# A written-out order for four engines: new tables for the middle of a Conformer block on one core

## The chip, the core and the metric

The kernel runs on one core of a Trainium2 chip. The core has five engines that run at the same time, each through its own list of instructions: TensorE (PE, matrix multiplies into PSUM), VectorE (DVE), ScalarE (ACT, the exponentials and tanh), GpSimd (POOL) and SyncE (SP, which issues transfers). They wait for each other only through semaphores. The metric is the device time of one execution, in microseconds (us). Before the change it is 867.25 us, the median of 3 runs (867.09 to 867.63).

## The reference, cut to what matters

Two sequences of 4000 tokens with 144 features go through one Conformer block: feed-forward, self-attention with 4 heads of 36, gated convolution, feed-forward, and a layer norm in front of each part and at the end.

```
x = x + 0.5 * (silu(layernorm(x) @ w_ff1a) @ w_ff1b)
q, k, v = split(layernorm(x) @ w_qkv)              # 4 heads of 36
p = softmax(q k^T / 6)                             # 4000 x 4000 for each head and sequence
x = x + (p v) @ w_o
a, b = split(layernorm(x) @ w_pw1)
c = depthwise 5-tap convolution of a * sigmoid(b)  # zeros beyond both ends
x = x + silu(c) @ w_pw2
x = x + 0.5 * (silu(layernorm(x) @ w_ff2a) @ w_ff2b)
return layernorm(x)
```

The exponentials of the scores are the largest part: 2 sequences x 4 heads x 4000 x 4000.

## The kernel before

**Tiles of attention.** Queries are taken in 16 chunks of 500, keys in steps of 64 (the last one has 32). One tile is one key step of one chunk, all four heads; there are 1008 of them, 16 of which are the short rests. The scores of a tile are four matmuls of 64x64 weights against 500 columns (`scores`, rows `PS<-QT,KT` of the profile); each uses one quarter of the array and four of them run side by side. They fill two PSUM banks. An exponential turns both banks into a bf16 tile `PT`, and four more matmuls (`PS<-PT,VA`) sum it with the values into the two banks `BX` and `BX + 1`, where column 37 is the sum of the softmax.

**Two ways to an exponential.** The letter of a tile in the table `TYPES` says who does it.

- `A`: one instruction on ACT over 1000 columns (`e_args`). `R` is the same for a rest, over 500 columns.
- `D`: DVE does it by bit arithmetic (`z_args`, `ymw_args`). Two instructions `z` of 500 columns turn scores into 16-bit integers whose high bits are the exponent. Then, over 1000 columns, `y` cuts out the mantissa, `m` multiplies, and `w` keeps the exponent. The tile becomes two buffers, `w` and `m`, and so eight matmuls with the values, not four.
- `W`: as `D`, with one `z` of 1000 columns.

Two such tiles can share `y`, `m` and `w`, each then of 2000 columns, where the table `PAIRS` names them. The long instruction starts when the `z` of both tiles are done.

**The other work.** For each chunk of 500 tokens there are the layer norms (statistics on DVE, `ST`; a scale-and-add of four numbers to a row, `RS<-ST`, on POOL or DVE; a power on POOL, `RS<-RS,NHALF`; the normalised rows `XN` on POOL, DVE or ACT), a transpose by a transfer (`XTB<-XN`), and full-array matmuls: feed-forward (`WA`, `WE`, `WB`), projections (`WQ`, `WK`, `WQKV`), output (`WO`), gate (`WP`, `WPZ`) and convolution (`DG`). Results leave PSUM through DVE or ACT: the copies `KT`, `QT`, `VA`; `HT` after a tanh on ACT; and the residual `X`. A residual on DVE is one instruction that adds to `X`. On ACT it is a plain copy, and two matmuls of `X` with an identity (`PS<-X,EYE`) add the old value before it.

**What sets the order.** Recording the program (`Rec.op`) yields blocks of instructions and their dependencies. `settle` then replaces all attention tiles by what the tables say, and `Rec.arrange` puts the blocks of each engine in exactly the order of the table `ORDER`, two characters for a block. The chip takes each engine's list in that order; an instruction that has to wait holds up all that stand behind it on its engine. The other tables:

- `UNITS`: one letter for each of 447 small pieces of work that more than one engine can do (`Rec.unit`, `Rec.choose`): `d` DVE, `a` ACT, `p` POOL.
- `BANKS`: the PSUM banks (0 to 5) of each tile. `PLACES`: the first bank of each other PSUM use.
- `SLOTS`: which of the 11 `PT` buffers each tile uses. A buffer or a bank is written again when its last reader, in PE's order, is through.

The order is thus made outside the kernel, by a search over a plan that gives each instruction a duration. What is in the kernel of that plan are the costs in `c_act`, `c_dve` and `c_pe`; the tables do not depend on them when the program is built.

```
def c_act(n):
    return n / 1200 + 0.0535
...
        R.choose(UNITS)
...
            m = lead.get(n)
            wide = () if m is None else tuple(parts[m][4])
...
        R.arrange(ORDER, readers, slots, users)
```

Of the kernel before, what the change touches and what calls it, by code (L numbers as in the profile page):

```python
# [13 lines left out]
H = 4  # L14
# [21 lines left out]
        '!!!#!$!%!&!(!+!)!*!,!-!.!/!0!1!3!6!2!;!5!4!<!=!7!8!A!9!:)c)d!@!>)g)h!B)l)k!?)p)o!C)w)x!D)t)s)r)m)n)e'  # L36
        ')|)i)j){!E!J!G!F!H*!)y)v)q)f)u!I!K!L!M!P!S!N!R!O!Q!T!U!`!V!W!b!X!Z!^!g!_!f!Y!d!j!a!c![*$*#!]!e!o!p!l'
        '!k!h*)*(!m*,*-!n)z*1*0!i!q*4*5*&*%*8*9!s!t*=*<)}*/*3*.*6*@*A!u!r!w!v*E*D!x*I*H!y*L*M*B*G*V*+*;*:*W*P'
        '*7*F*Q***2*K*Z*[*>*C*J!z*`*_!{!|!}*c*d*g*h#!##*q*?*m*n*T*U*}*Y*N*^*X*r#%#&*v*u*p*b*o#$*z*y*O*R+!*a*k'
        '*t+,+-*f*e#)+)+(*S*s#(+:+;+.*|*j*w+%*x+G*]+1+0+/+4*l*i#*+5*{+?+>+=+<+++F+B+C+*#+#,#-+L+M+Q+@+D+A+P+$'  # L40
        '+9+&+##.+[+Z+T+O+E+_+`+R+S+J+I+K+2+8+U+c+d+k+3+H+h+g+6+7+N+r+q#/+v+u+l+i+b+^+f+z+y+a,&+]+}+j,!+s+t+w'
        '+X,++e+x,%#0,1,0+{+Y,*,$+o+p,4,5#1,8,9+V#2,=,<,),2+m+W,G,#,7,F,A,@+n,:,3,6,K,J,(+|,>,;,/,,,N,O,H,S,I'
        ',.,R,-,?,Z#3,W,V,L,Q,M,P,b,a#4,f,e,[,X,U,T,Y,i,j#5,m,n,d,B,q,C,x,w#6,{,|,g,l,c,r-#-$#7-)-(,h,k,z-,,p'
        '-2-3,o#8-6-7,y-+-*,E-%-&-;-:,}-!,^,_,]---?->#9-C-B,u-K-<-9-=-8-F-G-4,`,D-1-P-Q,t-.,v-@-5-J-U-T-D-E-X'
        '-I-0-/-_-`-Y-A-H,s-d-c#<-g-h#:#;#>#?#=-k-l-o-b-p-e-f-w-j-N-W-i-V-O-t-s#@#A#B-x-a.!-}#C.&.%-L-S-R-M.*'
        '.+./-q-r.#-u-v...$#D#E.8.9-^.-.,.).<.=-]#F.@.A.;.3.:-m-n.D.E.0#G.1-{.I.H.2-z.>.?.(.L.M-|.P.Q-Z.K.B.^'
        '._-y.O.F-[.T.C.N.J.G.b.c.7.R.S.X.f.6.5.g.j.V.U.4.k.W#H#I.a.h.u.t.`.y.x.e.d.n.|.}#J.o.l.m.z/%.i/$.{/)'
# [12 lines left out]
        '56#{5=5%595:4_4o4^5D5C5>5350574n545/5X5W5<5G5+585N5M#|5F5`5;5H5Q5,5Y5Z5[5]5E5B5O5*5a5)#}5A5P5d5e5^5_'  # L60
        '5?5R5@5i5h$!5m5l$#5q5p5t5f5g6!5}5j5J5b5c5k5I5w6&6%5L5r5o5s5K5x5n5V5U6*6+5T5S5u5v$$6/6.6962$%686(636<'
        '6=$&$(6A6@6$6#6)$)6:6E6?6D656I666;6H$*61606S6R6,6C6L675z6B6W6V$+646M6F5|6Z6G6>6[6e6Y6U5{6f6X6_6-6T6K'
        '$,$-6j6i6^6m6g6]6n6N6O6J6h5y6`6P6w6x$.6q6p6{6Q6o6|6k6l6y6r7#7$$/7(7)$0$17-7,6}6b706d767!7%77$26a717&'
        '7.7;7:6v6u7>7E6z787/7D$37H7I7*7?797<7+6c7M7L$47Q7P7G7F6s6t7T7U$5$674757X7Y7]7S$77d7c7C7J7B7^7g7K7V7h'
        '7R7O7N737q7=7k7r$87v7u7f7i7j727e7l7z7y$97@7W8(8)7}7A7s7b7Z7[8,8-$:81807t7w8!7_7`8*8584$;8?8>83827p88'
        '7|7a8+8B8C7{$<8.8/8F8G8@89867x$=878J8K8D8A7o8&8N8E8H8U8T$>8X8Y7m8$8%8O8L8M8]8^$?8#8W7n8V8g8h8;8a8:8['
        '8Z8I8k8l$@8p8o8`8i8R8b8P8j8s8t$A8x8w8r8q$B8{9)9*8u8=8n9-8Q8<8y9.9!8v8S8m8|8}92918c8d8e8f8_8z96959#$C'
        '9?9@909/9C9D9,99$D9H9G94939:97989+9R9Q$E9F9&9U9V9B9E9K9(9Z9Y$F9_9^9S9L9J9A9$9c9b9%9I9f9]9T9[9l9m$G9p'
        '9q9=9e$H9t9u9X9W9g9`9a9d:#9O:!9>9;9<9r9x9o:(:&$I:,9M9y:$9N:+9P9n:5:6:/:%9j9s9k:::99v:0:.$J:=:*:>:-:B'
        ':)9h:A9}$K:L:E:K9z9{:?:8:7:@:4:O:C:P:3:F9i:<:;:T:S:M:D9w:W:^:_$L:2:X:b:c:U:R:V:G:a:f:N:g:1:H:`:j9|:q'  # L70
        ':p$M:k:I:u:t:d:J:[:e:s:|:i:x:y:r:];&;($N$O;-;.:Y:Z:}:Q;2;1$P;<;;:m:h:{;?;0:n:l;@;/;3:o;4;C;D;5:v;=$Q'
# [2471 lines left out]
```

## Time and profile before

| | us |
|---|---|
| median of 3 runs | 867.25 |
| lowest, highest | 867.09, 867.63 |
| the profiled execution, its device time | 867.84 |
| its span, first to last instruction | 865.7 |
| PE busy | 849.3 (98%) |
| ACT busy | 835.0 (96%) |
| DVE busy | 835.4 (96%) |
| POOL busy | 284.8 (33%) |

The granted TensorE clock was 0.999 in the profiled execution. All instructions of the kernel are issued from one helper line, so the rows are told apart by their tiles, such as `PT<-PS` for an exponential. "Busy" runs from the start of an instruction to the end of its result; the next one on the same engine can start before that end. How long an instruction holds its engine is therefore read from the distance of two starts, and a wait can hide in an instruction that only looks long. In the chain of waits, a piece is the part of an instruction that the end of the program depended on.

### The profile page before, as it was taken

What the parts mean: (1) busy time and instruction counts of PE and PEld (TensorE: products, weight loads), DVE (VectorE), ACT (ScalarE), POOL (GpSimd) and SP (SyncE); (2) the same over time, 40 slices, a digit from 0 to 9 for tenths busy, and PEclk for the clock granted to TensorE, in tenths of its full rate; (3) what the DMA queues carried; (4) which work ended last, traced back from release to release, by engine and by line L of the source; (5) the groups of instructions that cost most, each with busy time, mean ns of one, the idle gap of its engine ahead of it and who ended that gap; (6) DMA issues with size and microseconds to landing.
All of it is one profiled execution on the core that took longest, in us unless ns stands there. A gap on an engine that the chain in (4) does not pass through costs nothing.

```text
span 865.7 us, 27015 instructions
## 1 busy us (share of the span) xinstructions
PE 849.3 (98%) x11585; PEld 411.3 (48%) x11585; DVE 835.4 (96%) x1819; ACT 835.0 (96%) x1096; POOL 284.8 (33%) x562
## 2 busy tenths in 40 slices
PE   9999999999999999999999999999999999999996
PEld 7644434444344444444444444444444544445485
DVE  7999999999999999999999999999999999999987
ACT  6999999999999999999999999999999999999975
POOL 7771331041334301432230060230550163300854
PEclk9999999999999999999999999999999999999999
DMA  3331211102113110212210020010130021100121
GB/s 102 78 58 21 33 21 36 23 14 45 34 26 51 15 27 2 40 32 45 33 38 3 2 45 3 14 32 14 27 42 11 3 57 29 29 10 14 32 53 52
DMA packets 86330, 26.90 MB, mean 31 GB/s; under 512 B 81384, under 2 KB 86210, under 8 KB 86210
## 3 DMA queue, kind: packets, MB, share of 16 engines
q1 hardware_dynamic: 84662, 24.34, 15.4%
q8 instruction: 90, 1.47, 0.7%
q10 hardware_dynamic: 1548, 0.84, 0.4%
q14 instruction: 30, 0.25, 0.1%
HBM read 3.31 MB, written 2.30 MB: 6 GB/s over the span
## 4 chain that ended last, share of the span: by engine, by line
ACT 40%; PE 40%; DVE 16%; DMA 1%; POOL 1%; issue 0%; ACTq 0%; SPq 0%; DVEq 0%; POOLq 0%
PE PS L591 40%; ACT PT L591 37%; DVE PT L591 11%; ACT TH L591 3%; DVE ST L591 1%; DVE QT L591 1%; DVE X L591 1%; POOL XN L591 1%; DVE HT L591 1%; DVE U L591 1%; DMA XTB<-XN 1%; DMA X<-in_x_dram 0%; DMA WE<-in_w_ff1a_dram 0%; DVE KT L591 0%; ACT X L591 0%
## 5 line engine op out<-in xcount | busy, mean ns | idle before, releaser
L591 ACT ACTIVATE PT<-PS 128x1000 bf16<-128x1000 f32 (+1 forms) x793 | 729.9, 1071 | 4.9 <-PE PS L591 4.1
L591 PE MATMUL PS<-QT,KT 64*64 64x500 bf16 x3968 | 460.1, 383 | 4.3 <-ACT PT L591 1.2
L591 PE MATMUL PS<-PT,VA 64*37 64x500 bf16 x4828 | 449.7, 372 | 1.3 <-DVE QT L591 0.5
L591 DVE TENSOR_SCALAR PT<-PS 128x500 int16<-128x500 f32 x425 | 279.1, 676 | 4.4 <-PE PS L591 3.1
L591 PEld LDWEIGHTS PS<-QT,KT 64*64 64x64 bf16 x3968 | 139.8, 104 | 201.7 <-ACT PT L591 99.2
L591 PEld LDWEIGHTS PS<-PT,VA 64*37 64x37 bf16 x4828 | 163.1, 96 | 105.7 <-issue 16.4
L591 POOL TENSOR_SCALAR RS<-ST 125x4 f32<-125x4 f32 (+1 forms) x132 | 31.2, 238 | 479.3 <-DVE ST L591 475.4
L591 DVE TENSOR_SCALAR PT<-PT 128x1000 uint16<-128x1000 uint16 x430 | 172.2, 418 | 1.7 <-DVE PT L591 0.2
L591 DVE TENSOR_TENSOR PT<-PT 128x1000 bf16<-128x1000 bf16 x215 | 144.4, 676 | 0.8
L591 POOL TENSOR_SCALAR XN<-X,RS 125x144 bf16<-125x144 bf16 x246 | 141.1, 587 | 3.8 <-POOL RS L591 0.5
L591 POOL TENSOR_TENSOR RS<-RS,NHALF 125x4 f32<-125x4 f32 (+2 forms) x93 | 92.4, 998 | 50.1 <-DVE RS L591 48.0
L591 ACT ACTIVATE TH<-PS 128x500 bf16<-128x500 f32 (+3 forms) x175 | 92.7, 559 | 3.8 <-PE PS L591 3.3
L591 PE MATMUL PS<-XTB,WA 72*128 72x500 bf16 (+2 forms) x280 | 71.3, 359 | 1.1 <-DMA XTB<-XN 0.4
L591 DVE SCALAR_TENSOR_TENSOR HT<-TH,PS 128x500 bf16<-128x500 bf16 (+1 forms) x120 | 71.2, 614 | 1.1 <-ACT TH L591 0.8
L591 DVE BATCH_NORM_STATS2 ST<-X 125x6 f32<-125x288 bf16 (+1 forms) x160 | 65.6, 448 | 2.2 <-DMA X<-in_x_dram 1.6
L591 DVE SCALAR_TENSOR_TENSOR X<-PS,X 125x288 bf16<-125x288 f32 x114 | 50.7, 450 | 7.2 <-PE PS L591 6.2
L591 PE MATMUL PS<-WB,HT 128*125 128x144 bf16 (+1 forms) x640 | 52.2, 229 | 0.0
L591 PEld LDWEIGHTS PS<-WB,HT 128*125 128x125 bf16 (+1 forms) x640 | 44.9, 136 | 13.5 <-issue 3.9
L591 PEld LDWEIGHTS PS<-XTB,WA 72*128 72x128 bf16 x280 | 21.5, 97 | 29.5 <-issue 8.3
L591 PE MATMUL PS<-U,DG 128*128 128x375 bf16 (+7 forms) x204 | 28.0, 263 | 0.1
L591 POOL COPY U<-U 128x2 bf16<-128x2 bf16 (+1 forms) x54 | 10.9, 236 | 42.2 <-DVE U L591 32.0
L591 ACT ACTIVATE HT<-PS 128x500 bf16<-128x500 f32 (+3 forms) x43 | 20.6, 537 | 3.4 <-PE PS L591 2.9
(98 smaller groups left out, 523.1 us busy)
## 6 DMA issues: line engine op xcount, KB each, us to landing
X<-in_x_dram SPq DMA_DIRECT2D x16, 140.6 KB
XTQ<-XTB SPq DMA_DIRECT2D x24, 70.3 KB
out_dram<-XN SPq DMA_DIRECT2D x9, 140.6 KB
XTB<-XN SPq DMA_TRANSPOSE x53, 3.8
out_dram<-PT SPq DMA_DIRECT2D x3, 140.6 KB
out_dram<-PT ACTq DMA_DIRECT2D x2, 140.6 KB
XTB<-AN SPq DMA_TRANSPOSE x15, 3.2
WA<-in_w_ff1a_dram ACTq DMA_DIRECT2D x1, 144.0 KB
```

Source lines behind the costliest of these rows:

```text
L591: ins = getattr(eng, o.name)(*o.a, **o.k)
```

## The change

Only tables change; no function does. Read through the blocks that the tables stand for, this is the difference:

- `TYPES`: tile 356 (chunk 5, key step 41) goes from `W` to `A`. The other 1007 letters stay.
- `PAIRS`, empty before, names two pairs: tiles 277 and 280, and tiles 482 and 485, all of type `D`. Each pair issues `y`, `m` and `w` once over 2000 columns where each tile issued them over 1000.
- `UNITS`: 22 of 447 letters. Thirteen `RS<-ST` of layer norms go from POOL to DVE and two the other way. Four residuals go from ACT to DVE (on ACT they start at 211.13, 320.55, 422.85 and 629.81 us of the profile), and with them eight `PS<-X,EYE` matmuls go. One `KT` copy of 500 columns goes from ACT to DVE (at 112.58 us). One `VA` copy of 72 columns goes from ACT to DVE and another from DVE to ACT.
- `BANKS`: 11 of 2016 digits. `PLACES`: 3 of 1721. `SLOTS`: 745 of 2016.
- `ORDER`: of the blocks that both kernels have, 3718 of 5043 stand at another place on PE (by 58 places at most), 562 of 1671 on DVE (22 at most), 144 of 310 on POOL (11 at most), 31 of 99 on SP (4 at most) and 20 of 1083 on ACT (2 at most). Up to 60 us and from 814 us on, PE, ACT, DVE and POOL have the same lists.
- PE's order alternates between quarter-array matmuls and other kinds: 689 changes of kind before, 704 after. The full-array work lies in 295 runs before and 302 after.

```diff
 ORDER = {
     "pe": (
-        '!!!#!$!%!&!(!+!)!*!,!-!.!/!0!1!3!6!2!;!5!4!<!=!7!8!A!9!:)c)d!@!>)g)h!B)l)k!?)p)o!C)w)x!D)t)s)r)m)n)e'
+        '!!!#!$!%!&!(!+!)!*!,!-!.!/!0!1!3!6!2!;!5!4!<!=!7!8!A!9!:)_)`!@!>)c)d!B)h)g!?)l)k!C)s)t!D)p)o)n)i)j)a'
...
 TYPES = (
...
-    'AAAADAADAAAAARDAAAADAAADAAAAADAAADAADAAAADAADAAADAADAAADWAADAADAAAAADAAAAAARDAADAAAAAAADAADAADAAAAAA'
+    'AAAADAADAAAAARDAAAADAAADAAAAADAAADAADAAAADAADAAADAADAAADAAADAADAAAAADAAAAAARDAADAAAAAAADAADAADAAAAAA'
...
 SLOTS = (
-    '(!!!*!-!#!$!)!!!*!+!#!(!$!,!%!+!)!-!$)&!*!+!!!(#,!)!&!,!%-!!+!+!&!$!(!$!*),!%!$+(!-!!!)!#(%!,!*!)!,!'
+    '(!!!*!-!#!$!)!!!*!+!#!(!$!,!%!+!)!-!$)&!*!+!!!(#%!*!,!&!)+(!%!!!-$,!*!%!#)!!+!$%,!&!*!+!#!-!(!,!)!*!'
...
 UNITS = (
     'ppdddapddddpddddaddddaadaaadappaaapdppddddddppdddpddadddpdpaadaaadaapddpdpppddpdpdadadddppdddppadadd'
-    'daddddddddddpddppdddadaadadddpddppppddppddppddddddppdppdddppaaappdadddddppppdddadddppddppddddadddppd'
...
+    'daddddddddddpdddpdddadaadddddpddppdpddppdddpdddddddpdppdddppdaappdadddddppdpdddadddppdddpddddadddppd'
...
 PAIRS = (
+    (277, 280), (482, 485),
 )
```

More of the change, by code (lines that the diff above doesn't have):

```diff
@@ new lines @@
+        '*o+)+(*t*g#)+#+$*e*p*s*f*J*K+7+6#(*h+*+,+C*x*a+-+0*|#*+1*{+:+;+.+/*}+++!+B+>+?#+#,#-+I+H+8+%+M+@+L+9'
+        '#.+=*w+W+5+V+P+Z+[+4+O+F+G+E+<+N+Q+_+`+D+K+g+3+&+2+c+d+A+J+m+n#/+q+r+X+Y+h+b+a+]+f+u+v,!+p+o+y+z+e+s'
+        '+^+T,&+}+t#0,-,,+w+U,%+|+k+l,0,1#1,4,5+R#2,9,8,C,.+{+x,$+i+S,B,/,6+j,<,3,2,F,G,=,:,+,#,(,7,J,K,O,*,D'
+        ',E,N,),;,V#3,S,R,I,L,M,H,W,],^#4,a,b,U,P,T,Q,e,f#5,j,i,`,>,?,m,s,t#6,x,w,h,_,n,c,{,|#7-$-#-(,l,v,g,k'
+        ',d-.-/#8-2-3-!-%,u,}-)-6-7-&,X,y,z-;,Z-1-:,Y-B#9-?->,@,o-0-C-8-5-4,A-F-=-<-M-L-G,p-,,[-@,r,q-P-Q-A-9'
@@ new lines @@
+        '---T-Z-[-U-+-D-*-E-`-_#<-d-c#:#;#>#?-e-b-g-h#=-S-k-s-l-f-J-R-K-a-^-o-p#@#A#B-]-t-y-z#C-}.!-H-n-q-I.%'
+        '.&-m-r.*-i.+#E#D-X-Y.5.4.(.)-|-N.9.8#F./-{.<.=-O-w.6.7.@.A#G.D.E.:-x.,.--W...I.H.$.L-v.>.B-j.#.M.G.C'
+        '.Y.Z.;.f.P-u.K.O.^._.F-V.?.3.b.N.1.2.T.c.J.Q.R.0.g.S#H#I.a.t.p.q.`.u.h.e.j.d.y.x#J.r.k.s.}.|.X.i.{.W'
+        '/$.V/%.U/).w.v.z.]///0#K/4/3/#.[/(/!/&/*/7/8#L/</;#M/E.m/?.o/1/F/5/J.l/>/=/2/I/6/@.n#N/M/N/G/H/Q/L/Z'
+        '/9/R/+#O/V/U/Y/./-/:#P/`/j/i/S/K/B/W/,/n/m#Q/r/q/A/D/X/C/c/P/|/{/T/O/[/d/^/]0#0$/u/_/b/a0/0.#R030(02'
@@ L161 @@
+        '$p$k$q$|$w$x$y$t$v$j$u$z${$}%!%#%%%$%0%&%(%1%)%*%+%,%-%.%2%3%/%5%6%4%7'
     ),
@@ L202 @@
[L202 to L205 removed]
+        '!!!#!$!%!&!*!,!(!.!)!0!+!2!-!/!4!6!5!1!8!7!3!9!<!B!;!C!=!:!>!@!A!?!D!E!F!w!M!H!N!G!J!I!L!K#4!O##!Q!T'
@@ L206 @@
+        '%B%C%A%D%E%F%G%H%I%K%J%L'
     ),
     "sp": (
[L208 to L209 removed]
+        '!!!#!%!&!(!$!)!*!+!,!-!2!.!/!0!1!3!5!4!6!7!9!:!8!<!=!>!?!@!;!B!A!C!D!E!F!G!H!I!J!K!O!L!Q!P!R!N!M!S!V'
+        '!T!U!W!X!Y![!]!^!`!Z!a!e!b!_!f!g!c!h!i!d!m!j!k!o!n!p!q!r!l!t!s!u!v!y!z!w!}!|!x!{#!#%#&###$#(#*#)#+'
@@ new lines @@
+    '$!&!%#,!#!$!+!&)(!!!-!*!(!+&,!)!-!)&!!#!$!,(%!!!$!+!-!*+#!%!!$(!-!#!)!(!&!,#+!%!$(-!)!%!!&+!*!&!-!#)'
+    ',!+!*!+!%,-!(!$!+&!!(!-!#!-!!!(#*!%!-!,!%!+!!!$!)**!+!-!#!&!-%,!$!+!&+(!*!#!!)*!$!(!%!-*#!$!)!&-+!,!'
+    '(!!,*!)!#!-&$)%!+!!**)%!)!+-$!#!(!,!&!)!$!,!#!(!-!)!+!%!,!-!#!*+&!%!)!(!$!)!!!+!%),!(!!(#!-!&!(!$!-!'
+    '%#&!,!+!&!%!*)$!,!&!$!+!#!,!&!(!-#)!%!&!#*$!(-,!+!&!,!!!&%)!%!$!*!#!$(+!*!)!,!#!)!+#&$-!%!,!*-!!)!(!'
+    '%)-!,!#!&+!!$!(!#!$!!(,!-!)+$!,!#!%*-!*!,!#$(!-!,!)+(!-!&!!,*!(!&*-!%!(-(!)!$!,!%!!!)!,!#!+!$!#*%!&!'
@@ new lines @@
+    '!!)!%!$!,$-!+!)!%&*!#!(!!&)!+!(+-!*!)!*(,!#!$!-!%)&!)!$!*$,!-!&!!!#-+!(!,!&!(!-)$!#!*!,*+!#!)%!+(!&!'
+    '-!$,(!#!&!(!-)*!)!&!%&#!!!*!(!+!%!$%&!#!)!(!+!,!-!%!)#&!,!(!$!&%*!-!+!!!#+(-,!)!$!!*%!*!)!&!,-$!+!)!'
+    '&!#%(!)!$!)!,(+!-!!!*%&!#!)#$)-!+!(!%#!!&!!+-!,!(!*!-!#!&!(!#*%!-!+!&!,!(!)!$!%*-!(!+!$!&!-!(!(&,!*!'
+    '%!#+)!,!-!)!%&!!*!)!(!,!(&$!#!-!*!+,!!%!$!!!)#-!,!*!+&(!!!$!-,#!&!$!%*(!)&,!+!(!,!&!#!#(-!)!+!$!&(%!'
+    '!!,!)+-!$!+!%!*%&!(!!!-!,-#!!!$!+!*!-*&!!!(!$%%!#!+!,!)(!!#!*!-%,!+!#!*+(!!!)!&%$!#!!!+),!#!$!(!*!!!'
@@ new lines @@
+    ',!&!(!$+%!)!*,-!#!+!%!!!)!+-*$$!#!&!%!(!,!)!+!-!&!%$$!#!(,+&)!!!*-&!#!)!!!)(-!,!%*!!+!$!!+,!#!-!$!&!'
+    '*!,)(!$%%!+!-!#!&!!!+!-,(!%!*!&!!!#,$!!*%!)!$!-!+%,!#!(!$&&!)!-!,!(**!-!#!)!-,%!!!+!)!!)#!&!+!%!$+#!'
+    ')!,!*--!&!#!,!(!&!%$,!(!!!+$)!#!-!*!,&&!#!!!*+-!#!%!(!)-#!$!+!!!&*(!,!%!#!$*+!-!)!!!%#(!,!)!+!($!!-!'
+    '*!)$&!!-,!(!%!+(#!*!%!,!!!,*-!#!(!%!&!$+#!(!)!!!-%,!&!())!#!,+&!!!&)*!+!-!-&$!%!(!#!$!(!%!!*)!,!+!#!'
+    ',!-!$!)!+!(!#*%!!!-!$!&!)#!!$!+!!!-(,#$!)!%!!!*+&!#!-!,+$!*!(!%#)!$!-!-!(!!!&*#!!!$!(!$!,!-!(!&!)+$!'
@@ L290 @@
+    '#!%!$!)-*!#!*#,!'
 )
```

359 lines of the change are left out of this document (164 added, 195 removed).

## The prediction

> **What bounds the kernel now.** I read the page first, then the stretches of time, then ScalarE's groups between 60 and 812 us, where the change lies.
>
> ```profile
> PE 849.3 (98%) x11585; PEld 411.3 (48%) x11585; DVE 835.4 (96%) x1819; ACT 835.0 (96%) x1096; POOL 284.8 (33%) x562
> ...
> ACT 40%; PE 40%; DVE 16%; DMA 1%; POOL 1%; issue 0%; ACTq 0%; SPq 0%; DVEq 0%; POOLq 0%
> ```
>
> Three engines look full, and the chain that ended last goes back and forth between them. No engine is alone the bound: an engine's saved work is worth its share of this chain, unless it lies in a stretch where that engine is the chain. The stretch that the change reaches and the one behind it (columns: PE, PEld, DVE, ACT, POOL busy):
>
> ```profile
> 60.00:812.00 752.00, 744.33 (x10323) 337.37 (x10324) 739.05 (x1543) 745.29 (x927) 206.24 (x403) 1.00 0.15 26
> 812.00:866.00 54.00, 46.97 (x548) 34.78 (x540) 43.05 (x133) 39.54 (x80) 31.19 (x57) 0.97 0.22 50
> ```
>
> The end, where engines really idle, keeps its order. In the 752 us between, ACT shows only 6.7 us (752 - 745.29) without an instruction. But a wait can hide in a long instruction, so I count ACT's work from distances of starts. ACT's groups of that stretch, and single rows of ACT that give the paces:
>
> ```profile
> L591 ACT ACTIVATE PT<-PS 128x1000 bf16<-128x1000 f32 x748 | 696.0, 1081 | 4.1 <-PE PS L591 3.3
> L591 ACT ACTIVATE TH<-PS 128x500 bf16<-128x500 f32 x97 | 61.8, 653 | 0.5 <-PE PS L591 0.4
> L591 ACT ACTIVATE PT<-PS 128x500 bf16<-128x500 f32 x15 | 10.0, 667 | 0.0
> L591 ACT ACTIVATE TH<-PS 128x250 bf16<-128x250 f32 x18 | 8.4, 464 | 0.5 <-PE PS L591 0.4
> L591 ACT ACTIVATE X<-PS 125x288 bf16<-125x288 f32 x12 | 5.4, 449 | 0.9 <-PE PS L591 0.9
> ```
>
> ```profile
> 502.59 0.44 ACT L591 ACTIVATE X<-PS 125x288 bf16<-125x288 f32 x1
> 502.88 0.42 ACT L591 ACTIVATE TH<-PS 128x250 bf16<-128x250 f32 x1
> 503.14 8.23 ACT L591 ACTIVATE PT<-PS 128x1000 bf16<-128x1000 f32 x9
> 511.10 0.76 ACT L591 ACTIVATE TH<-PS 128x500 bf16<-128x500 f32 x1
> 511.57 1.19 ACT L591 ACTIVATE PT<-PS 128x1000 bf16<-128x1000 f32 x1
> ```
>
> Nine exponentials from 503.14 to 511.10 make 0.884 us for one; a 500-column instruction holds ACT 0.47, a 250-column one 0.26, a residual `X` 0.29. So ACT's work is 748 x 0.884 = 661.2, plus 123 of 500 columns (97, 15 and 11 copies) x 0.47 = 57.8, plus 18 x 0.26 = 4.7, plus 12 x 0.29 = 3.5, plus the 26 left of the 927 at no more than 0.26, 6.8. That is 734.0 of 752: **ACT is held for at least 18.0 us** in the stretch. This is what a better order can take at most. A page of the Trainium skill speaks against such room: by "ScalarE: Activation LUTs" (What ACT_TABLE_LOAD costs), an instruction of N columns takes 186 ns + 0.833 N and two in a row overlap by some 93 ns, by estimate 0.926 us for 1000 columns. By it 748 exponentials would be 693 us, the stretch would be full, and no order could gain: the time would stay as in the first rival below. The nine starts 0.884 apart contradict it here, so I leave 0.05 of my chances to it, within that rival.
>
> **The change part by part.** Rows for its prices: the chain where the `KT` copy leaves ACT, the chain where a residual does, PE around a residual, and one piece of full-array work between quarter-array matmuls.
>
> ```profile
> 111.50 0.68 DVE KT L591
> ...
> 112.58 0.59 ACT KT L591
> 113.16 0.90 ACT PT L591
> ```
>
> ```profile
> 319.21 5.80 PE PS L591 x81
> ```
>
> ```profile
> 204.81 11.17 PE PS L591 x158
> ```
>
> ```profile
> 422.49 0.42 DVE X L591
> ...
> 427.27 0.36 DVE X L591
> 427.63 0.58 DVE PT L591
> 428.22 0.59 DVE KT L591
> ```
>
> ```profile
> 210.80 0.29 PE L591 MATMUL PS<-X,EYE 125*125 125x144 bf16 x2
> 211.02 0.41 PE L591 MATMUL PS<-QT,KT 64*64 64x500 bf16 x4
> ```
>
> ```profile
> 109.85 2.06 ACT L591 ACTIVATE PT<-PS 128x1000 bf16<-128x1000 f32 x2
> ...
> 112.58 0.59 ACT L591 ACTIVATE KT<-PS 128x500 bf16<-128x500 f32 x1 [0.67 <-DVE KL L591]
> ```
>
> 1. *The `KT` copy goes to DVE.* On ACT it waits 0.67 us, and on the chain it holds the next exponential until 113.16, though the one before ended at 111.91 (109.85 + 2.06). The gain lies between its own 0.48 (half a microsecond of ACT) and 1.25. DVE has 0.59 more, behind which only its own next `z` waits. I take -0.9, nearest to wait and half the work.
>
> 2. *Four residuals go to DVE.* Each frees 0.29 on ACT, costs 0.37 on DVE (422.49 and 427.27 above) and saves PE two `EYE` matmuls, 0.22 (210.80 to 211.02). The one at 320.55 lies in a PE stretch of the chain (319.21), the one at 211.13 likewise (204.81); there it counts -0.22 each. At 422.85 DVE is the chain and it counts +0.37; the one at 629.81 I put there too. Sum +0.3; ends -0.9 (PE everywhere) and +1.5 (DVE everywhere).
>
> 3. *Tile 356 goes from DVE to ACT.* DVE loses `z`, `y`, `m`, `w` and ACT gets 0.884:
>
> ```profile
> 319.72 1.19 DVE L591 TENSOR_SCALAR PT<-PS 128x1000 int16<-128x1000 f32 x1
> ```
>
> ```profile
> L591 DVE TENSOR_SCALAR PT<-PS 128x1000 int16<-128x1000 f32 x5 | 6.0, 1193 | 0.1
> L591 DVE TENSOR_SCALAR PT<-PT 128x1000 uint16<-128x1000 uint16 x423 | 169.4, 418 | 1.7 <-DVE PT L591 0.2 <-PE PS L591 0.2
> L591 DVE TENSOR_TENSOR PT<-PT 128x1000 bf16<-128x1000 bf16 x211 | 141.4, 674 | 0.8
> L591 DVE TENSOR_SCALAR PT<-PS 128x500 int16<-128x500 f32 x413 | 268.8, 670 | 4.4 <-PE PS L591 3.1
> L591 DVE TENSOR_SCALAR RS<-ST 125x4 f32<-125x4 f32 x6 | 1.1, 182 | 0.1
> ```
>
> That is 2.7 us of DVE (1.193 + 2 x 0.418 + 0.674). It starts at 319.72, where PE is the chain, so both are covered by PE; PE itself saves four of the eight matmuls with the values, about 0.2 (four of 500 columns in 0.21, below). I take -0.2; without that cover it is +0.9 (ACT) or -2.7 (DVE).
>
> 4. *Two pairs.* Six instructions go. A `z` of 500 columns takes 0.670 and one of 1000 takes 1.193, so 0.15 of each does not depend on its length: six save up to 0.9 on DVE. Against it, the long `y` waits for four `z`, and four buffers of 11 stay taken longer. One pair stands near 424, where DVE is the chain: -0.3 for it, nothing for the other. If PE has to wait for the late sums, each pair can cost one `z` more, +0.7.
>
> 5. *Eleven `RS<-ST` (net) go to DVE*, at most 0.18 each, 2.0 in all; DVE is 16% of the chain: +0.3. POOL, 206 us busy of 752, gains nothing on the path.
>
> 6. *Seven more runs of full-array work on PE.*
>
> ```profile
> 209.02 0.37 PE L591 MATMUL PS<-QT,KT 64*64 64x500 bf16 x2
> 209.23 0.38 PE L591 MATMUL PS<-PT,VA 64*37 64x500 bf16 x4
> ...
> 110.89 1.00 PE L591 MATMUL PS<-XTQ,WK 72*128 72x500 bf16 x4 [0.31 <-issue]
> ...
> 304.13 0.60 PE L591 MATMUL PS<-XTB,WA 72*128 72x500 bf16 x2
> 304.65 0.40 PE L591 MATMUL PS<-QT,KT 64*64 64x500 bf16 x2
> ```
>
> Groups of quarter-array matmuls follow at 0.21 (209.02, 209.23). Two `WA` passes need 0.42 at that pace, and the scores behind them start 0.52 later: 0.1 for the way back. The way in costs between nothing and the 0.31 shown. So a run costs 0.1 to 0.4, seven 0.7 to 2.9, of which PE's 40% of the chain makes 0.3 to 1.2. I take +0.5.
>
> 7. *The order of PE and DVE.* This is most of the change, and no row prices it. Bound: the 6.7 us that ACT visibly idles in the stretch, all gone or as much again. The residuals and the copy that leave ACT are, with 0.67 here and the 0.9 of group `X` above, where ACT stood longest beside its exponentials. So the new tables act on waits that the chip really has, which is my reason to expect a gain. Those 1.6 us are a tenth of the 18.0; I take about the same again, rounded to **-2.0**, for the exponentials' own waits.
>
> 8. *Orders of POOL and SP, buffers, banks* add no instruction; I take nothing. POOL's waiting for statistics covers the first. If the cover of SP's order goes, one transfer like this one stands on the path, up to 4.4:
>
> ```profile
> 644.49 4.44 DMA XTB<-XN
> ```
>
> Sum: -0.9 + 0.3 - 0.2 - 0.3 + 0.3 + 0.5 - 2.0 = -2.3. The profiled execution took 867.84 (span 865.7) and would take 865.5; it is 0.6 over the median 867.25, so I forecast 867.25 - 2.3 = **865.0 us**.
>
> **The rivals.** *The order gives nothing.* The moved instructions are real, but the reordered blocks only exchange one engine's wait for another's: with 40% of the chain on PE and 16% on DVE, an exponential that is ready earlier waits for a bank. Then only items 1 to 6 are left, -0.3: 866.95 us. For it: ACT's own order hardly changes (20 of 1083 blocks). Against it: item 7.
>
> *PE becomes the bound, and it is slower.* If the waits of ACT that now cover PE's changes of kind go, every one counts: seven runs at 0.4 are +2.9, less 0.4 for the `EYE` matmuls in PE's stretches and 0.2 of tile 356: 869.5 us with nothing gained by order. It decides once PE is on the chain for some 75% of the stretch (0.75 x 2.3 = 1.7); now it is 40%. For it: PE is at 98%, and the pieces of background work get smaller. Against it: half of the wait into a run is hidden behind matmuls still streaming. The Trainium skill has a rule on this side: "TensorEngine Tiling (Array Packing)" (Key Properties) says that a change of tiling mode drains the engine. The idle 0.31 at 110.89 agrees with it; a full drain for each new run is what this rival counts.
>
> *The order gives most of what it can.* All 6.7 us of visible idle go: 867.25 - 0.3 - 6.7 = 860.3 us. Against it: the waits of DVE and PE in the same places would have to fall as well.
>
> **How the numbers follow.** About 0.2% (1.7 us) is what a measurement of this kernel can tell from no change. The forecast has 0.38, its own range 863.3 to 865.5; the large gain 0.08; both are faster, 0.46. The order that gives nothing has 0.26 (865.5 to 869.0). The slower rival has 0.28, as PE is so near its bound and a new order is only as good as the durations it was made with. Ends of the range: below 862.0 lies most of the large gain, above 869.6 the slower part beyond its price, 0.2 together.
>
> **What would show it.** Item 1: no `KT` copy of ACT near 112 and the exponential there some 0.9 us earlier. Items 2 and 3: `X` of ACT 14 to 10, `EYE` 24 to 16, wide `z` 5 to 4. Item 4: `y` and `w` of 2000 columns, 4 in all, at less than twice 0.418. Item 5: POOL's `RS<-ST` 11 fewer. Item 6: more weight-load idle put down to "issue" than the 74.9 us here:
>
> ```profile
> PEld PS L591 <- issue: 74.9, 245, 0.6
> ```
>
> Item 7: exponentials with a mean below 1081 ns, and ACT at 98% of a shorter stretch. The prediction is wrong if PE's share of the chain rises well over 40% while ACT's falls, or if the mean of the exponentials rises.

## The result, and the profile after

The changed kernel takes **869.67 us** (median of 7 runs, 869.31 to 871.03), the kernel before 867.02 on the same chip. The ratio is **1.0033**, with a 95% interval of 1.0021 to 1.0045: it is slower by 2.7 us, where 865.0 was forecast. Its profiled execution took 869.67 with a span of 867.6, so 1.9 more than the 865.7 of the profiled execution before, which at 867.84 was itself 0.8 above its median.

The lines of the changed kernel that answer to those of before: busy time and chain from the page, the stretch from 60 to 812 us (PE, PEld, DVE, ACT, POOL busy), ACT's groups in it, and what the weight loads wait for (total, times, longest).

```profile
PE 851.1 (98%) x11573; PEld 414.6 (48%) x11573; DVE 836.1 (96%) x1825; ACT 837.1 (96%) x1092; POOL 290.9 (34%) x551
...
PE 53%; ACT 30%; DVE 14%; DMA 2%; issue 1%; SPq 0%; ACTq 0%; DVEq 0%
```

```profile
60.00:812.00 752.00, 743.88 (x10282) 339.47 (x10284) 737.80 (x1545) 745.39 (x921) 211.00 (x390) 1.00 0.15 26
```

```profile
L592 ACT ACTIVATE PT<-PS 128x1000 bf16<-128x1000 f32 x747 | 694.6, 1056 | 5.9 <-PE PS L592 4.6
...
L592 ACT ACTIVATE X<-PS 125x288 bf16<-125x288 f32 x8 | 3.6, 445 | 0.0
```

```profile
PEld PS L592 <- ACT PT L592: 92.9, 295, 0.8
PEld PS L592 <- issue: 80.6, 260, 0.8
PEld PS L592 <- DVE PT L592: 75.3, 233, 0.9
...
PEld PS L592 <- DVE HT L592: 16.9, 44, 1.0
PEld PS L592 <- DVE X L592: 8.5, 25, 0.6
```

The same waits before:

```profile
PEld PS L591 <- ACT PT L591: 107.5, 334, 0.8
...
PEld PS L591 <- DVE PT L591: 71.7, 236, 0.6
PEld PS L591 <- DVE HT L591: 13.2, 39, 0.7
...
PEld PS L591 <- DVE X L591: 5.9, 19, 0.5
```

Read them like this. Weight loads wait 14.6 us less for ACT. They wait 3.6, 3.7 and 2.6 more for DVE's `PT`, `HT` and `X`, and 5.7 more for "issue" (74.9 before): the wait changed its owner, it did not go away. The chain left ACT (40 to 30%) for PE (40 to 53%).

The fall of the exponentials' mean from 1081 to 1056 ns looks like a gain, and the prediction had named it as one. It is a loss. An exponential shows as long when it starts while the one ahead still runs (one that starts after idle time shows 1.00 in the rows below), and it can start so only when its scores are ready early. From the starts of the 607 exponentials in the stretch that follow directly on another, one comes 0.902 us after the other before, and 0.908 after; so the overlap shrank from some 0.18 to 0.15. With less than 0.13 of overlap there were 162 of the 607, now 270. The part of each distance above 0.885, summed, is 10.5 us before and **14.4 after**: 3.9 us more in which ACT stands between two exponentials.

Place by place (the start of the same block of ACT in both traces, each counted from its first matmul) the gains stand where they were forecast: 0.5 where the `KT` copy left ACT, 0.3 at the residual near 210, and 0.2 around tile 356. Against them stand steps up where no instruction changed its engine: +0.46 at 67, +0.2 at 124, +0.25 at 272, +0.3 at 440, 508 and 808 each. These belong to the new order and not to one execution. The traces of nopairs, after_rs and lead_a, which keep that order, have those at 67, 124, 440, 508 and 808 within 0.1 of the same size; moves, kt_behind, x_places and lead_b, which keep the old one, show less than 0.02 there. Not every step is of that kind: the changed kernel also gains 0.5 near 649, where PE before waited 0.40 for a transfer (`XTB<-XN`), and moves, kt_behind, x_places and lead_b, with no edit there, are 0.2 to 0.5 shorter at that place too.

### The profile page after: what moved, and what is told of

Its sections match the earlier page's. It is cut to its first block, busy times and chain, and to the rows that moved or that the text cites. A ratio compares the mean times of both kernels' runs of the same rounds, so it can differ in the third digit from the quotient of the medians.

```text
span 867.6 us, 26980 instructions
## 1 busy us (share of the span) xinstructions
PE 851.1 (98%) x11573; PEld 414.6 (48%) x11573; DVE 836.1 (96%) x1825; ACT 837.1 (96%) x1092; POOL 290.9 (34%) x551
## 4 chain that ended last, share of the span: by engine, by line
PE 53%; ACT 30%; DVE 14%; DMA 2%; issue 1%; SPq 0%; ACTq 0%; DVEq 0%
PE PS L592 53%; ACT PT L592 27%; DVE PT L592 10%; ACT TH L592 3%; DVE ST L592 1%; DVE QT L592 1%; DVE HT L592 1%; DMA XTB<-XN 1%; DMA X<-in_x_dram 0%; DVE U L592 0%; DVE X L592 0%; DMA WE<-in_w_ff1a_dram 0%; DMA XTQ<-XTB 0%; DVE AN L592 0%; DVE SW L592 0%
## 5 line engine op out<-in xcount | busy, mean ns | idle before, releaser
L592 DVE TENSOR_SCALAR PT<-PS 128x500 int16<-128x500 f32 (+1 forms) x424 | 278.2, 675 | 3.9 <-PE PS L592 2.0
L592 POOL TENSOR_SCALAR XN<-X,RS 125x144 bf16<-125x144 bf16 x246 | 145.8, 606 | 4.9 <-POOL RS L592 0.5
L592 DVE TENSOR_TENSOR PT<-PT 128x1000 bf16<-128x1000 bf16 (+1 forms) x212 | 143.8, 682 | 1.0
```

Source lines behind the costliest of these rows:

```text
L592: ins = getattr(eng, o.name)(*o.a, **o.k)
```

## The experiments

The times in the expectations count from the first matmul; the profile's rows show the same moments some 1.5 us later. Each ratio is to runs of the kernel before on the same chip (866.4 to 866.8 us there). Orders are shown decoded: a number is a step of other work, `S31` the scores of tile 31 (with `.0` or `.1` for one half), `z88.1` the second `z` of tile 88, `O` value sums.

**Moves and order apart.** The change has two parts that can be made one at a time: instructions go to other engines, and the blocks get another order.

```
moves:       UNITS, TYPES of after; ORDER, BANKS, SLOTS, PLACES of before;
             a moved block stands where it started before:
  DVE  ... 1555  + KT copy (1547)  z88.1 ...
order_units: the reverse: ORDER, BANKS, SLOTS, PLACES, TYPES of after, UNITS of before,
             PAIRS = ()
nopairs:     after with PAIRS = (), y, m, w of 280 and 485 behind those of 277 and 482
```

> The old orders, buffers and banks, and every instruction that the change moves to another engine on its new engine (KT, four X, tile 356, the RS steps, two VA pieces), no pairs; each moved instruction stands where it started before. PE has 630 changes of kind as before. Theory 'the new order costs': what the moves give stays and nothing is lost: 865.0 to 866.2 us (the steps down that the two traces show at the moved instructions sum to -2.4, not all of them reach the end), that is -0.8 to -2.0. Rival 'the moved work itself costs (DVE too full)': 868.5 us or more. Rival 'PE's extra changes of kind cost': also below 866.5, as they are not in this kernel.

> The new orders, buffers and banks of all engines with every step on its old engine (only tile 356 keeps its new type) and no pairs. PE has the 646 changes of kind of the changed kernel. Theory 'the new order costs': 869.5 to 871.5 us, +2.5 to +4.5, more than the whole change, as the gains of the moves are missing. Rival 'the moved work costs': 866.5 to 867.5, no change. Rival 'only the extra changes of kind cost': 16 changes, 8 runs at 0.25 us, 868.5 to 869.2.

> The changed kernel without its two pairs: tiles 280 and 485 have their own y, m and w again, put behind those of 277 and 482. If the late sums of the pairs cost what the price in the prediction bounds (+0.7 each), 868.2 to 868.6, 1.1 to 1.4 below the changed kernel. Theory 'the order costs, the pairs do not': within 0.4 of the changed kernel, 869.3 to 870.1.

Measured: moves alone 868.83 us, ratio 1.0031 (1.0020 to 1.0042); order alone 872.25, 1.0073 (1.0061 to 1.0086); without pairs 869.95, 1.0044 (1.0031 to 1.0056). Order alone costs 5.8 us, even more than the order theory had said. But moves alone cost 2.3, where a gain was expected, so that theory was too simple: each part loses without the other, and together they lose 2.7, not the 8.1 of their sum. The 868.83 of moves is what the rival "DVE too full" had named; the cut of DVE's work below (9 us less of it gain 1.3) speaks against that reason. In both kernels the moved blocks stand where their old start times put them, and no search placed them, so a part of each loss may be the placing. And a part of order_units is a transfer: PE waits 1.3 us for `XTB<-XN` at 726, and against the changed kernel ACT steps up by 1.0 there. The pairs gain some 0.9 of the changed kernel, with an interval that reaches past zero; in the traces it is one step of 0.85 at 269, where in nopairs value sums wait 0.50 for DVE's tile. What the traces show of the gain is thus the pair's place in this order, not its shorter instructions.

Why moves alone lose is seen at the `KT` copy. ACT's rows in the kernel with moves alone (start, length, kind, count, idle time ahead and its releaser):

```profile
112.26 1.00 ACT L591 ACTIVATE PT<-PS 128x1000 bf16<-128x1000 f32 x1 [0.70 <-PE PS L591]
114.01 3.69 ACT L591 ACTIVATE PT<-PS 128x1000 bf16<-128x1000 f32 x4 [0.75 <-PE PS L591]
```

and DVE's:

```profile
112.25 0.67 DVE L591 CAST KT<-PS 128x500 bf16<-128x500 f32 x1
112.83 0.67 DVE L591 TENSOR_SCALAR PT<-PS 128x500 int16<-128x500 f32 x1
```

Against the exponentials ahead of it, the one at 112.26 is 0.45 earlier than it was, as item 1 said (up to here the rows of this trace are 0.35 earlier than those of before, by a difference at their start, where nothing was edited). But the `z` behind the copy now starts at 112.83, and it frees the bank that the scores of tile 90 need; so their weight loads wait, and ACT stands 0.75 us ahead of the exponential at 114.01:

```profile
113.55 0.11 PEld L591 LDWEIGHTS PS<-QT,KT 64*64 64x64 bf16 x4 [0.89 <-DVE PT L591]
```

Gain 0.45, loss 0.87, one tile apart. Near 210, 423 and 630 the moved `X` show the same: 0.12, 0.13 and 0.25 gained, and 0.22, 0.39 and 0.35 lost one or two tiles later.

**Is it the place in DVE's list?**

```
kt_behind: DVE  ... 1555  z88.1  + KT copy (1547) ...    (nothing else moved)
x_places:  the same, and  z217.0 y214 z216.0 + X 2707 | y351 m351 + X 4059 |
           z485.0 + X 5290 | z763 + X 7699;  TYPES[356] = A
```

> The kernel before with one instruction moved: the KT copy of 111.06 us goes to DVE, behind the z of tile 88, where the changed kernel has it, and not ahead of that z, where the run 'moves' had it. There ScalarE's next tile came 0.45 earlier, and the one behind it 0.43 later than before, as DVE's z freed its PSUM bank late. Theory 'the place in DVE's order decides': no loss at 112.4; 0.4 to 0.5 earlier from there on, the end 0.3 to 0.5 below the kernel before on the same chip (ratio 0.9994 to 0.9996). Rival 'DVE has no room there, wherever it stands': +0.3 to +0.5 as in 'moves'.

> The kernel before with the moves that shorten ScalarE's work, each a block or two later in DVE's order than in 'moves': KT behind z of tile 88, the four X behind z of 216, m of 351, z of 485 and z of 763; tile 356 goes to ScalarE. The RS steps and the two VA pieces stay. Theory 'the place decides': 0.45 at KT and 0.1 to 0.25 at each X stays, no later loss, the end 0.6 to 1.2 below the kernel before. Rival 'the DVE work itself costs': 0.5 above it or more, as in 'moves' (+1.0 of span).

Measured: kt_behind 866.64, ratio 1.0003 (0.9994 to 1.0012); x_places 869.77, 1.0037 (1.0025 to 1.0050). ACT's rows of kt_behind:

```profile
111.97 1.00 ACT L591 ACTIVATE PT<-PS 128x1000 bf16<-128x1000 f32 x1 [0.63 <-PE PS L591]
113.14 3.69 ACT L591 ACTIVATE PT<-PS 128x1000 bf16<-128x1000 f32 x4 [0.16 <-PE PS L591]
```

The place counts: the wait of 0.75 became 0.16. Yet 0.41 came back five tiles on, and the whole is neither faster nor slower: the 0.4 to 0.5 expected did not reach the end. For the residuals the place mattered the other way. Put behind a `z`, three of the four cost about a microsecond each (+0.83 at 212, +0.97 at 424, +1.19 at 630; the one put behind an `m` shows no step), as the residual itself keeps a PSUM bank that scores wait for:

```profile
425.33 0.11 PEld L591 LDWEIGHTS PS<-QT,KT 64*64 64x64 bf16 x2 [1.04 <-DVE X L591]
```

```profile
423.77 1.90 ACT L591 ACTIVATE PT<-PS 128x1000 bf16<-128x1000 f32 x2 [0.21 <-PE PS L591]
426.63 1.90 ACT L591 ACTIVATE PT<-PS 128x1000 bf16<-128x1000 f32 x2 [0.97 <-PE PS L591]
```

So "a later place is better" falls; what stands is that a moved block is worth what its bank and the block behind it allow.

**One piece of order, and one block.**

```
w56_80: before, with after's order, banks and buffers for blocks between 56 and 80 us
fix31:  after's PE order  ... O30 S31.0 [+ S31.1] S36.1 O27 O22 [- S31.1] S32.0 ...
```

> The kernel before, with the new order, buffers and banks only for the blocks between 56 and 80 us, where the change moves no instruction to another engine. Theory 'a block in PE's order stands ahead of a tile that ScalarE needs, and waits for a late bank': the step seen at 66.7 us in the changed kernel, +0.46, appears here alone, and the end is 0.3 to 0.5 later: 867.4 (span 866.1 to 866.2). Rival 'DVE's instructions were only slow by chance there, or the moved instructions later on cause it': no step at 66.7, 867.0.

> The changed kernel with one block moved in PE's order: the second half of tile 31's scores, which ScalarE needs next, goes ahead of a score of tile 36, which waits for a bank that DVE frees late. Theory 'head of the line': ScalarE's tile 31 starts 0.3 to 0.5 earlier and the step of +0.46 at 66.7 us goes; the end 0.3 to 0.5 below the changed kernel (ratio to before 1.0027 in place of 1.0033). Rival: tile 36 on DVE gets late in its turn and the step comes back behind it, no change at the end.

Measured: w56_80 869.69, ratio 1.0038 (1.0025 to 1.0050); fix31 869.47, 1.0035 (1.0023 to 1.0048). w56_80 settles nothing about the step of 0.46: the two orders do not fit at the edges of the window, and the trace shows +0.9, +1.4 and +1.0 there. fix31 tests the head of PE's line. ACT's rows in the changed kernel, and then with S31.1 ahead:

```profile
68.70 1.00 ACT L592 ACTIVATE PT<-PS 128x1000 bf16<-128x1000 f32 x1 [0.55 <-PE PS L592]
69.60 0.58 ACT L592 ACTIVATE KT<-PS 128x500 bf16<-128x500 f32 x1
70.07 1.91 ACT L592 ACTIVATE PT<-PS 128x1000 bf16<-128x1000 f32 x2
```

```profile
67.96 1.00 ACT L592 ACTIVATE PT<-PS 128x1000 bf16<-128x1000 f32 x1 [0.34 <-PE PS L592]
68.86 0.58 ACT L592 ACTIVATE KT<-PS 128x500 bf16<-128x500 f32 x1
69.52 1.90 ACT L592 ACTIVATE PT<-PS 128x1000 bf16<-128x1000 f32 x2
```

The wait at tile 31 fell from 0.55 to 0.34, but from the `KT` copy to the next exponential it is now 0.66 in place of 0.47: the rival was right, the step came back behind it.

**PE's changes of kind.**

```
merge: before's PE order, 20 pieces moved later, e.g.
   S645  - 6622 6628  S646  + 6622 6628  6641 6648 6678 ...
```

> The kernel before with 20 pieces of full-array work on PE moved later, up to the next such piece, where their readers have time for it by the trace (at least 0.08 us to spare): 596 changes of kind in place of 630, 17 runs fewer, nothing else. Theory 'a change of kind costs 0.25 to 0.4 us a run and PE is the bound': 4 to 6.5 us less. By PE's 40% of the chain: 1.7 to 2.7 less. Theory 'what counts is which tile stands ahead, not the changes': within 0.5 of the kernel before, or slower where a reader gets late.

Measured: 870.59, ratio 1.0046 (1.0033 to 1.0058). With 17 runs of full-array work *fewer* it is 4.1 us slower. PE's rows of before at one of the places, and then of merge (the bracket is idle time and its releaser):

```profile
541.12 0.60 PE L591 MATMUL PS<-U,DG 128*128 128x500 bf16 x3
541.68 0.41 PE L591 MATMUL PS<-QT,KT 64*64 64x500 bf16 x4
```

```profile
541.19 0.65 PE L591 MATMUL PS<-QT,KT 64*64 64x500 bf16 x6
542.33 0.41 PE L591 MATMUL PS<-QT,KT 64*64 64x500 bf16 x4 [0.49 <-ACT PT L591]
542.66 1.25 PE L591 MATMUL PS<-U,DG 128*128 128x500 bf16 x9
```

Before, the piece at 541.12 filled the time in which the scores behind it waited for their bank. Moved away, it left 0.49 empty, and its own time was added later. At this place, then, a change of kind was free, as PE waits for a bank there anyway. But merge does not price the changes of kind alone, as it also makes the readers of the moved work late. The tanh that reads this convolution, before and then in merge, starts 6.21 and 6.48 us after the first of the seven exponentials ahead of it:

```profile
536.83 6.59 ACT L591 ACTIVATE PT<-PS 128x1000 bf16<-128x1000 f32 x7
543.04 0.86 ACT L591 ACTIVATE TH<-PS 128x500 bf16<-128x500 f32 x1
```

```profile
537.47 6.59 ACT L591 ACTIVATE PT<-PS 128x1000 bf16<-128x1000 f32 x7
543.95 0.60 ACT L591 ACTIVATE TH<-PS 128x500 bf16<-128x500 f32 x1
```

Counted from distances of starts in the stretch, ACT stands 1.3 us longer directly ahead of a tanh in merge than before, 1.6 longer directly behind one, and 0.1 longer between exponentials. So its loss stands beside the tanhs, which read full-array work, and whether fewer changes of kind gain anything by themselves stays open.

**What is an engine's time worth?** The same small cut all over the middle of the kernel, one engine at a time. These kernels do not compute the columns that are cut.

```
 # in replay, from tile 60 on
 trim_act:  a = (a[0][:, :, 0:490], a[1][:, :, 0:490]) + tuple(a[2:])     # the exponentials
 trim_dve:  z: 0:490 of 500;  y, m, w: 0:980 of 1000
 trim_pe:   a, k = (a[0][:, 0:486],), dict(k, rhs=k["rhs"][:, 0:486])     # scores and sums
 _b: in the kernel before; _a: in the changed kernel
```

> The kernel before with 980 of 1000 columns in each exponential of ScalarE from tile 60 on (726 of them; 20 columns of each tile are left as they were in the buffer). At the slope between 500 columns (0.47) and 1000 (0.884) that is 16.6 ns each, 12.0 us of ScalarE. By its 40% of the chain of before: 4.8 us less (ratio 0.9945). Rival 'ScalarE alone is the bound': near 12 less. Rival 'three engines are so near each other that work taken from one alone gives next to nothing': less than 2.

> The kernel before with 490 of 500 columns in each z, and 980 of 1000 in each y, m and w, of VectorE's tiles from 60 on (402 z, 206 of each other; the columns left out stay as they were). 4.2 us for the z by the slope between 500 (0.670) and 1000 columns (1.193), at most 3.4 for y and w and 2.8 for m: 8 to 10 us of VectorE. By its 16% of the chain: 1.3 to 1.7 us less (ratio 0.998). Rival 'VectorE is as much a bound as the others, the chain shows it too small': 3 us less or more.

> The kernel before with 486 of 500 columns in each quarter-array matmul from tile 60 on (8280, four at a time: 2070 groups of 0.2105 us at 500 columns, 5.9 ns less each; the other columns of scores and sums are left out). 12.2 us of PE. By its 40% of the chain: 4.9 us less (ratio 0.9944). Rival 'PE at 98% is the bound': 9 to 12 less. Rival 'near each other': less than 2.

> The same cut of PE's matmuls (486 of 500 columns from tile 60 on, 12.2 us of PE) in the changed kernel. Theory 'the new order has made PE the bound' (53% of its chain): 6.5 us less than the changed kernel or more, so about 863.0, and clearly more gain than the same cut gives the kernel before. Rival 'the new order loses at waits of ScalarE and DVE, not at PE': the same gain as in the kernel before or less.

> The changed kernel with 980 of 1000 columns in each exponential of ScalarE from tile 60 on (12.0 us of ScalarE; the other columns are left out). In the kernel before the same cut gave 4.3 us (0.36 of it). Theory 'the new order leaves ScalarE waiting for others': less, 3.5 or below (its chain share 30% gives 3.6), so 866 or more on a chip where the kernel before takes 866.5. Rival 'ScalarE's time is dearer in the new order': 5 us or more.

> The changed kernel with 490 of 500 columns in each z and 980 of 1000 in each y, m and w of VectorE's tiles from 60 on, without the two pairs (8 to 10 us of VectorE; the columns left out stay as they were). In the kernel before this gave 1.4 us. Theory 'VectorE has become dearer, as its late z, HT and X now hold PE': 2.5 us or more, so below 867. Rival 'as in the kernel before': 1.2 to 1.6 us.

Measured (gain: ratio times 866.5 us, for the changed kernel against its 1.0033; worth: gain by us cut). The cuts are the estimates of the expectations, with DVE's taken as 9. In the traces an exponential then follows 17 ns sooner (884 to 867), a group of four matmuls 5 (213 to 208), a `z` 10, an `m` 11, a `y` or `w` 5; so DVE's cut is rather 8, and its worth before 0.16.

```
              cut us   ratio (95%)               gain us   worth
trim_act_b     12.0    0.9950 (0.9937..0.9962)    4.3      0.36
trim_dve_b      9      0.9985 (0.9976..0.9993)    1.3      0.14
trim_pe_b      12.2    0.9985 (0.9976..0.9994)    1.3      0.11
trim_act_a     12.0    1.0007 (0.9999..1.0016)    2.3      0.19
trim_dve_a      9      1.0015 (1.0006..1.0024)    1.6      0.17
trim_pe_a      12.2    1.0012 (1.0004..1.0021)    1.8      0.15
```

Before, the chain's shares were near as prices for ACT (0.40 against 0.36) and DVE (0.16 against 0.14), and far off for PE (0.40 against 0.11). The chain of trim_pe_b, and of trim_act_b:

```profile
ACT 48%; PE 31%; DVE 20%; issue 1%; POOL 0%; DVEq 0%; POOLq 0%; ACTq 0%
```

```profile
PE 55%; DVE 26%; ACT 17%; issue 1%; DMA 0%; POOL 0%; DVEq 0%; ACTq 0%
```

The share passes to the others as soon as one engine is relieved. In the changed kernel PE has 53% of the chain, and 12.2 us less of it buy only 1.8: PE has not become the bound there. ACT's time is cheaper than before (2.3 against 4.3, with intervals that just overlap), which agrees with the 3.9 us that ACT now stands between exponentials. The three worths sum to 0.61 before and 0.51 in the changed kernel. No run cut all three engines at once; that may buy more than the sum, as each cut alone leaves the other two as they are.

**Which moves matter in the new order?**

```
after_rs: after, with the 15 RS steps that changed between POOL and DVE put back
after_x:  after, with KT, four X and two VA steps back (125, 160, 202, 207, 232, 251, 315 of UNITS)
```

> The changed kernel with its 15 RS steps and small VA steps that changed between POOL and VectorE back on their old engines (11 net back to POOL, 2.0 us of VectorE), all else as changed. By 0.15 for each us of VectorE: 0.3 less than the changed kernel. Theory 'VectorE is dear in the new order': 1 us less or more. Rival 'each block put back by hand costs a wait': 0.3 to 1 more.

> The changed kernel with KT, the four X and the two VA steps back on their old engines (four X with their EYE matmuls on PE again), each where it would start by time; all else as changed. The run with all units and the pairs put back was 5.8 us over the kernel before, 2.3 over the one with the pairs alone put back. If these seven steps carry that, 1.5 to 2.5 over the changed kernel, and RS put back carries nothing; at 0.36 for each us of ScalarE (2.1 us more there: KT 0.47, four X 0.29, two VA against each other) only 0.8.

Measured: after_rs 868.67, ratio 1.0025 (1.0015 to 1.0035); after_x 873.92, 1.0088 (1.0074 to 1.0102). The RS steps on DVE cost the changed kernel some 0.7, less than an interval tells apart. Without the seven others the new order is 4.8 slower, where moves and x_places lost by them in the old one. But not all of this is shown to be theirs. The trace of after_x is 4.0 longer than that of the changed kernel, and steps of 2.9 stand at 723 to 725, where none of the seven is. PE waits there for a transfer for which it does not wait in the changed kernel:

```profile
726.23 0.66 PE L592 MATMUL PS<-XTB,WA 72*128 72x500 bf16 x2 [1.51 <-DMA XTB<-XN]
```

The transfer lands 4.8 us after its issue there, and 3.2 after it in the changed kernel. order_units shows the same wait (1.32). Why it lands later was not tested.

**Scores earlier.**

```
lead_a (after), lead_b (before):  PE  ... - O O  S(n).0 S(n).1  + O O ...   at 31 and 29 tiles
```

> The changed kernel with 31 pairs of scores of ScalarE tiles each one group of four matmuls earlier in PE's order, ahead of two value sums whose readers have 0.3 us or more to spare; only where the bank was free by then and the scores were ready less than 0.4 us ahead. Theory 'scores stand too late in the new PE order': fewer exponentials with under 0.13 us of overlap than 270, and 0.5 to 1.5 us less than the changed kernel (ratio to before 1.0016 to 1.0027). Rival 'the sums then come late and hold their buffers': no change or slower.

> The kernel before with 29 pairs of scores of ScalarE tiles moved ahead in PE's order by the same rule. Same theory: 0.3 to 1 us less than the kernel before (0.9989 to 0.9997), which would beat both. Rival 'in the old order the scores stand where they have to, and any shift of a block costs': 0.5 us more or worse, as the pieces moved together (+4) and the X put later (+3) did.

Measured: lead_a 869.87, ratio 1.0035 (1.0023 to 1.0047); lead_b 866.94, 1.0003 (0.9994 to 1.0012). Nothing came of either. The exponentials with under 0.13 us of overlap only went from 270 to 259, so this rule does not repair the new order. That the thin overlap is the cause and not a sign of it is not shown, and moves speaks against it: the part of its distances above 0.885 sums to 14.8 us, as much as in the changed kernel, with 170 thin overlaps of 611.

No version that does the whole work ran faster than the kernel before; kt_behind and lead_b cannot be told from it.

## Why the prediction was wrong

The step that failed is **item 7, "the order of PE and DVE", -2.0**. The order alone measured +5.8, and on top of the moves +0.3 (869.67 to 867.02 against 868.83 to 866.5); the last is within the noise of two such ratios, and in no run did the order give a gain. Its reason, that the new tables act on waits which the chip really has, was right for the waits named there and said nothing of the others. The `KT` wait and the `X` waits went. The exponentials' own waits, of which I expected "about the same again" to go, grew by 3.9 us. As a sum over the changed kernel: ACT's work falls by 0.8 (0.48 and four times 0.29 less, 0.88 of tile 356 more), the waits of 0.67 and 0.9 go, and 3.9 come: +1.5 of the span's +1.9. The sign of being wrong that the prediction named by the chain came (PE 40 to 53%, ACT 40 to 30%); the sign by the exponentials' mean pointed the other way.

Point by point:

- *Item 1, KT, -0.9*: at its place -0.5 in the changed kernel, the low end. The cover named ("behind which only its own next `z` waits") was the error: behind that `z` waits a bank, and behind the bank a score and an exponential. In the old order the end of it is +0.2 with an interval of about 0.8 either way (kt_behind).
- *Item 2, four X, +0.3*: in the old order the steps of three of them sum to +0.46, and the fourth shows none. Right in size there, but by the bank and not by DVE's 0.37.
- *Item 3, tile 356, -0.2*: no step in the old order. In the new one -0.3 just ahead of it, and -0.2 once its own exponential and the residual that left ACT beside it are counted in.
- *Item 4, pairs, -0.3*: -0.9, with an interval from about -2.4 to +0.5. In the traces it stands at the pair that I priced at nothing (0.85 at 269); the one near 424 shows no such step. The instructions of 2000 columns were shorter than twice the others, as said (first line `y` and `w`, second `m`):

```profile
L592 DVE TENSOR_SCALAR PT<-PT 128x2000 uint16<-128x2000 uint16 x4 | 2.8, 710 | 0.1
...
L592 DVE TENSOR_TENSOR PT<-PT 128x2000 bf16<-128x2000 bf16 x2 | 2.4, 1187 | 0.0
```

- *Item 5, RS, +0.3*: +0.7, not told apart from it. DVE has 17 of them in the stretch, 6 before.
- *Item 6, more changes of kind, +0.5*: the sign that was named came ("issue" 74.9 to 80.6). The price was too high: PE's time is worth 0.11 to 0.15, not its 40%, so by estimate seven runs of 0.1 to 0.4 cost 0.1 to 0.4 in all.
- *Item 8, nothing*: the chain of before has the transfer at 644.49. The changed kernel's chain has two others:

```profile
420.63 4.52 DMA XTB<-XN
...
426.04 2.48 DMA XTQ<-XTB
```

The same two stand on the chain of lead_b, which keeps the old order, and PE itself waits 0.3 for an `XTQ` transfer, 0.2 before; so no cost of theirs is shown. In order_units and after_x a transfer did hold PE, by 1.3 and 1.5. SP's and POOL's orders were not tried by themselves.

The rival "PE becomes the bound", 869.5 us, gave nearly the measured number by a wrong reason. Its own condition, PE on the chain for 75%, is not met (53%), and the cut of PE shows that PE's time is cheap. By the Trainium skill, "TensorEngine Tiling (Array Packing)" (Key Properties), a change of tiling mode drains the engine. The idle 0.31 of PE at 110.89 agrees. At 541.12, by the rows of merge, the change cost nothing, as PE would have waited there anyway. "The order gives nothing" was nearer in kind, but it had the moves gain by themselves, which in the runs they did only in the new order.

What stays open: by which of its choices the new order is worse. A search by a plan's durations made it, and the traces show only where it waits. That its plan lays scores too close to the exponentials was argued, and lead_a did not confirm it.

## What to carry to other kernels

Where three engines are busy for 96 to 98% and feed each other through few buffers, a share of the chain is no price; cut a per cent or two of each engine's work and see what the time does. An instruction that leaves the busiest engine takes its PSUM bank and its place in a queue along, so follow it two steps on: who is behind it, which bank that one frees, and who waits for the bank. And a mean duration that falls in a row of back-to-back instructions can mean that the work behind arrives later, not that it got faster.

## What the runs showed of the hardware

A DVE instruction on 16-bit data in SBUF can get longer while POOL is at work. Of the `y` and `w` of 1000 columns in the kernel before, 305 that POOL overlapped by under 30% of their length took 410 ns on average, and the 125 others 439, twenty of them over 500; the `z`, which reads PSUM, showed no such difference (671 and 668). One such case stands at the step of +0.3 in the changed kernel that starts at 440 us by the first matmul, 442 in the rows (a `y` or `w`, which mostly takes 0.41, and POOL's rows there):

```profile
442.86 0.63 DVE L592 TENSOR_SCALAR PT<-PT 128x1000 uint16<-128x1000 uint16 x1
```

```profile
441.43 1.80 POOL L592 TENSOR_SCALAR XN<-X,RS 125x144 bf16<-125x144 bf16 x4
443.17 1.23 POOL L592 COPY U<-U 128x2 bf16<-128x2 bf16 x4
```

The Trainium skill, "SBUF — State Buffer", (Summary: rules for kernel authors) says that when a DVE instruction is in a mode that takes both ports, or has two inputs in SBUF while GpSimd's instruction reads SBUF, the later of the two is blocked fully until the first is through. The sign agrees, and the traces do not show in which mode a `y` or `w` runs. But of the 113 that started while a POOL instruction was running, 56 took 0.411 or less, no more than usual, so a full block is not the rule here. All twenty over 0.5 started while POOL made `XN`; the 38 that started beside the power on `RS` took 411 ns on average. It is not what made the change slower: the changed kernel has 136 such instructions with a mean of 435.
